# Three of four early weight conversions moved from the middle of an attention stage to its last steps

## The chip, the cores and the metric

One core of one Trainium2 chip runs the whole program. The metric is the device time of one execution in microseconds (us), less is better; the median of several runs is given.

## The reference

Sliding-window attention with four sink keys (2 batches, 8 heads, 768 positions, head size 64, window 128) is followed by two feed-forward layers over the 1536 tokens (512 wide, 2048 hidden). In short:

```python
keep = is_sink | in_window                      # 4 sinks, or 0 <= row - col < 128
x = softmax(where(keep, q @ k.T / 8, -1e9)) @ v # -> [1536, 512]
h = maximum(x @ w_in1, 0);  x = (h * h) @ w_out1
h = x @ w_in2;              out = (h * tanh(softplus(h))) @ w_out2
```

Inputs are drawn as 64-bit floats for the weights and 32-bit floats for q, k and v.

## The kernel before

**Attention.** A tile is one block of 128 rows of one batch (12 tiles); a pair is one tile and two heads, so there are 48 pairs, numbered 0 to 47. One loop over n from -3 to 51 (line 541) runs a software pipeline: in step n the scores of pair n+4 are made on PE (`emit_s`), their row maximum is taken on VectorE, DVE (`emit_max`, line 367), the exponentials of pair n+3 come from ScalarE, ACT (`emit_exp`, line 379), and in even steps the sums of the pairs n+1 and n+2 are inverted on DVE (`emit_rs`, lines 390 and 391) and multiplied in on GpSimd, POOL (`emit_norm`, line 399). PE transposes the probabilities (lines 407, 408; they are copied out of PSUM by DVE where the pair is the first of its tile, else by ACT, line 415) and multiplies them with the values (`emit_av`, line 428). When the last pair of a tile has gone through, the tile's output is split into a high and a low part: ACT writes `xh` (`emit_x`, line 477), then DVE writes `xl` (`split_x`, line 483). The output accumulates in a PSUM tile `av` that has a single buffer, so the first value matmul of the next tile waits for `xl` of the tile before. From step 44 on no new scores are made: steps 44 to 51 are the drain.

**Weights.** A weight block (128 hidden units of one matrix) arrives as 512 KB of 64-bit numbers in `raw` (three buffers) and is turned into two 32-bit parts by a `Conv` object. Its steps are: `load` (a DMA on SP's queue), `head_pool` (one POOL instruction, line 131), `mid_r` (two DVE instructions, lines 137 and 141), `mid_or` (one on DVE, line 147), `high` (one on ACT, line 162) and `low_pool` (one on POOL, line 166). A step's scratch comes from five buffers of 2 KB per partition. Four blocks are converted within attention: `wi` and `wo` of hidden block 0, then of hidden block 1 (conversions 0 to 3 below). Conversion m starts with its load at step 5 + 9m, and its other steps follow 5, 7, 8, 11 and 12 steps later.

**Feed-forward layers.** `moe` runs 96 slots of 24 matmuls: 12 of the first product (line 620, tile `h`) and 12 of the second (line 636, tile `o`), one slot behind. Slot 0's first product needs conversion 0, slot 1's first product conversion 2; the second products of slots 0 and 1 need conversions 1 and 3. In slots 0 to 13 two further blocks are converted per slot, with `head` on ACT (line 129), `mid` on DVE, `high` on ACT and `low` on DVE. The raw blocks for these are fetched three ahead, as soon as one of the three `raw` buffers is free.

**Order.** Both stages stand under `tc.manual_schedule()`: in the trace each engine's instructions of one stage run in the written order, in order and blocking. Instructions of the second stage, however, stand between those of the first where the built program put them: rows of line 620 appear on PE in the middle of the drain. Within a step the conversions come last (lines 598 to 601): what a conversion puts on DVE in step 44 or 45 stands ahead of `emit_rs` and `split_x` of step 46.

```python
for m, x in enumerate(blocks):
    step = CONV_STEPS.get(n - CONV_AT[0] - CONV_AT[1] * m)
    if step:
        getattr(x, step)()
```

Of the kernel before, what the change touches and what calls it, by code (L numbers as in the profile page):

```python
# [28 lines left out]
def kernel(  # L29
# [42 lines left out]
    def load_limits():  # L72
        for j, src in enumerate((n_sink, window)):
            nc.scalar.dma_start(out=raw_i[:, j, :], in_=src.bitcast(I32).partition_broadcast(1))

    def limits(ps):
        nc.vector.scalar_tensor_tensor(
            out=lim1, in0=raw_i[:, :, 1], scalar=4294967296.0, in1=raw_i[:, :, 0].bitcast(U32),
            op0=ALU.mult, op1=ALU.add,
        )  # L80
        nc.vector.tensor_scalar(lim1, lim1, 0.0, float(S), op0=ALU.max, op1=ALU.min)
        nc.tensor.matmul(ps, lhsT=one, rhs=lim1, start=True, stop=True)
        nc.vector.tensor_copy(lim, ps)
# [111 lines left out]
    def load_tile(t, names="qkv", halves=1):  # L195
        if t >= len(tiles):
            return
        b, i = tiles[t]
        hs = H // halves
        for nm in names:  # L200
            dst = {"q": qn, "k": kn, "v": vn}[nm]
            dst[b, i] = apool.tile([P, H, D], F32, tag=nm + "n", name=nm + "n", bufs=5 if nm == "v" else 3)
        for h in range(0, H, hs):
            for nm in names:
                src, dst = {"q": (q, qn), "k": (k, kn), "v": (v, vn)}[nm]
                nc.sync.dma_start(
                    out=dst[b, i][:, h : h + hs, :],
                    in_=src[b, h : h + hs, i * P : (i + 1) * P, :].rearrange("h p d -> p h d"),
                )
# [16 lines left out]
    def positions():  # L226
        make_identity(nc, ident)
        for dst, base, pattern, mult in (
            (rel, 0, [[-1, P]], 1), (col, 0, [[1, P]], 0), (relp, P, [[-1, P]], 1)
        ):  # L230
            nc.gpsimd.iota(
                dst, pattern=pattern, base=base, channel_multiplier=mult, allow_small_or_imprecise_dtypes=True
            )
            if dst is rel:
                nc.gpsimd.affine_select(
                    out=rel, in_=rel, pattern=pattern, base=base, channel_multiplier=mult,
                    compare_op=ALU.is_ge, fill=1.0e9,
                )
# [4 lines left out]
    def first_mask():  # L243
        outside(nc.vector, m_cur, rel, win_ap)
        nc.vector.scalar_tensor_tensor(
            out=mask0, in0=col, scalar=ns_ap, in1=m_cur, op0=ALU.is_ge, op1=ALU.mult
        )
# [17 lines left out]
    def load_vsink(b):  # L265
        vc[b] = apool.tile([P, D], F32, tag="vc", name="vc", bufs=2)
        nc.sync.dma_start(out=vc[b], in_=v[b, :, 0:SK, :])
# [26 lines left out]
    def prep(t, which, half=None):  # L294
        if t >= len(tiles):
            return
        b, i = tiles[t]
        js = slice(0, NPAIR) if half is None else slice(half * NPAIR // 2, (half + 1) * NPAIR // 2)
        src = (qn if which == "q" else kn)[b, i]
        pt = ps_p.tile([P, NPAIR, P], F32, tag="pt", name="tr")  # L300
        for j in range(js.start, js.stop):
            nc.tensor.transpose(  # L302
                pt[:, j, :], src[:, 2 * j : 2 * j + 2, :].rearrange("p h d -> p (h d)"), ident
            )
        if which == "q":
            if half in (None, 0):
                for d, nm in ((qh, "qh"), (ql, "ql")):
                    d[b, i] = apool.tile([P, NPAIR, P], F32R, tag=nm, name=nm, bufs=2)
            hi, lo = qh[b, i], ql[b, i]
        else:  # L310
            p0 = kpos(i)
            hi, lo = kh[:, :, p0 : p0 + P], kl[:, :, p0 : p0 + P]
        hi, lo, pt = hi[:, js], lo[:, js], pt[:, js]
        nc.scalar.copy(hi, pt)  # L314
        st["prep"] = (pt, hi, lo)
# [169 lines left out]
    blocks = []  # L485
# [1 line left out]
        wt[0, fb] = weight_tiles(w1pool, fb)  # L487
        blocks += [Conv(conv, 0, fb, part, wt[0, fb]) for part in ("wi", "wo")]
    WARM = (6, 3, 2, 1)
    CONV_AT = (5, 9)  # L490
    CONV_STEPS = {0: "load", 5: "head_pool", 7: "mid_r", 8: "mid_or", 11: "high", 12: "low_pool"}

    NPR = len(pairs)
    with tc.manual_schedule():
        load_limits()
        nc.scalar.preload_act_table_set("natural_log_exp_and_others")
        load_tile(0, "qk", halves=2)
        load_tile(1, "qk")
        load_tile(2, "kq")
        load_tile(0, "v")  # L500
        load_tile(3, "kq")
        positions()
        load_tile(1, "v")
        load_vsink(0)
        load_tile(2, "v")
        load_tile(3, "v")
        warm = apool.tile([P, P], F32, name="warm")
        nc.vector.memset(warm, 0.0)
        nc.vector.memset(one, 1.0)
        nc.gpsimd.memset(two, 2.0)  # L510
        for x in sums:
            nc.vector.memset(x, 1e-9)
        idle = ps_a.tile([P, P + 2], F32, tag="av", name="idle")

        def keep_warm(times):
            for _ in range(times):
                nc.tensor.matmul(idle[:, 0:P], lhsT=warm, rhs=warm, start=True, stop=True)  # L517

        keep_warm(WARM[0])
        limits(idle[:, P : P + 2])  # L520
        first_mask()
        prep(0, "q", 0)
        place_prep()
        keep_warm(WARM[1])
        prep(0, "k", 0)
        place_prep()
        keep_warm(WARM[2])
        emit_s(*pairs[0])
        emit_max(*pairs[0], 0)
        emit_max(*pairs[0], 1)  # L530
        prep(0, "q", 1)
        place_prep()
        prep(0, "k", 1)
        place_prep()
        emit_s(*pairs[1])
        emit_max(*pairs[1], 0)
        emit_max(*pairs[1], 1)
        second_mask()
        window_masks()
        emit_exp(*pairs[0])  # L540
        for n in range(-3, NPR + 4):
            at = {d: pairs[n + d] for d in range(-3, 5) if 0 <= n + d < NPR}
            last = {d for d in at if at[d][2] == NPAIR - 1}
            t, j = divmod(n, NPAIR)
            if 4 in at and n > -3:
                emit_s(*at[4])
            if 3 in at and n > -3:
                emit_exp(*at[3])
            if n % 2 == 0:
                group = [at[d] for d in (1, 2) if d in at]  # L550
                if group:
                    emit_rs(group)
                for p in group:
                    emit_norm(*p)
                    if p[2] == NPAIR - 1:
                        emit_sink(*p[:2])
            if -3 in last:
                emit_x(*at[-3][:2])
            if 4 in at and n > -3:
                emit_max(*at[4], 0)  # L560
                emit_max(*at[4], 1)
            split_x()


            if n % 2 == 0:
                if n >= 0:
                    prep(t + 2, "kq"[j // 2])
                for d in (-1, 0):
                    if d in at:
                        emit_t(*at[d])  # L570
                if -1 in last:
                    emit_sink_t(*at[-1][:2], st["s", *at[4]][0] if 4 in at else None)
            else:
                for d in (-3, -2):
                    if d in at:
                        emit_av(*at[d])
                if -2 in last:
                    emit_sink_mm(*at[-2][:2])
            if -1 in at:
                evac_t(*at[-1])  # L580
            if n in (-3, -2):
                prep(1, "qk"[n + 3])
            place_prep()
            evac_sink()
            if n >= 0 and j == NPAIR - 1:
                load_tile(t + 4, "q", halves=1 + (t + 5 == len(tiles)))
                load_tile(t + 4, "k")
                load_tile(t + 4, "v")
            if n == -1 or (n >= 0 and t < len(tiles) - 1 and (t % NB, j) == (NB - 1, 2)):
                sink_keys()  # L590
            if n < 0:
                keep_warm(WARM[3])
            if n == 1:
                fast_flag()
                load_vsink(1)
            if n in (5, 13):
                spread_vsink(n // 8)
            for m, x in enumerate(blocks):
                step = CONV_STEPS.get(n - CONV_AT[0] - CONV_AT[1] * m)
                if step:  # L600
                    getattr(x, step)()
    att.close()


# [421 lines left out]
```

## Time and profile before

| | |
|---|---|
| runs | median 633.4 us of 3 (633.07 to 634.25) |
| the profiled execution | 634.14 us, its span 632.4 us |
| busy share of the span | PE 99%, PE weight loads 82%, DVE 73%, ACT 58%, POOL 11% |
| chain that ended last | PE 96%, DVE 2%, ACT 1% |
| granted TensorE clock | 0.999 of full speed (the upper of its two levels) |

The span runs from the first to the last instruction; the profiled execution takes 1.7 us more than its span. Attention fills the first 106 us, the feed-forward layers the rest, in a steady alternation of 2.72 us of line 620 and 2.72 us of line 636. PE's busy share is modelled at the ends of its matmuls, so waits are better read from the distance between starts. A bracket at the end of a timeline row gives the idle time ahead of it and what ended it.

### The profile page before, as it was taken

To read this page: it belongs to the slowest core of one execution; us is meant where nothing else is said; L and a number is where in the kernel's file an instruction comes from. 1 tells how busy PE (TensorE), PEld (TensorE's weight loads), DVE (VectorE), ACT (ScalarE), POOL (GpSimd) and SP (SyncE) were. 2 spreads that over 40 slices of the span, in tenths; PEclk is the share of its full clock that TensorE was granted. 3 is DMA by queue.
4 is the path that set the end of the run, shared out by engine and by line. 5 is a ranking of instruction groups with operands and counts; after the bars stand their busy time and mean duration, and the time that the engine had idled before them with its cause. 6 is when DMAs were issued, how large, how long until landed. Compare 5 with 4: busy or idle time off the path is not lost.

```text
span 632.4 us, 9265 instructions
## 1 busy us (share of the span) xinstructions
PE 624.2 (99%) x3382; PEld 515.9 (82%) x3382; DVE 461.9 (73%) x968; ACT 363.7 (58%) x745; POOL 71.1 (11%) x97
## 2 busy tenths in 40 slices
PE   8999999999999999999999999999999999999996
PEld 7778787888888888888888888888888888888885
DVE  5988983999852011138889869999888888888884
ACT  5988985777744333347777745555454444544442
POOL 4686773000000000000000000000000000000000
PEclk9999999999999999999999999999999999999999
DMA  8644630666630000005666600000010000010001
GB/s 200 148 118 104 164 120 26 195 204 201 199 101 1 2 0 1 0 1 169 197 199 199 192 10 1 0 2 1 1 66 1 1 1 1 1 67 0 2 0 69
DMA packets 61189, 46.83 MB, mean 74 GB/s; under 512 B 38996, under 2 KB 55636, under 8 KB 61140
## 3 DMA queue, kind: packets, MB, share of 16 engines
q1 hardware_dynamic: 60848, 45.82, 25.0%
q8 instruction: 27, 0.44, 0.3%
q10 hardware_dynamic: 292, 0.39, 0.2%
q14 instruction: 22, 0.18, 0.1%
HBM read 43.06 MB, written 3.15 MB: 73 GB/s over the span
## 4 chain that ended last, share of the span: by engine, by line
PE 96%; DVE 2%; ACT 1%; issue 0%; DVEq 0%
PE h L620 41%; PE o L636 41%; PE s L356 4%; PE av L428 3%; PE tr L302 2%; PE pt L408 1%; PE pt L407 1%; PE idle L517 1%; PE av L464 1%; DVE s L367 1%; ACT pr L379 0%; DVE cv_a L147 0%; DVE cv_r L137 0%; ACT kh L314 0%; DVE cv_r L141 0%
## 5 line engine op out<-in xcount | busy, mean ns | idle before, releaser
L620 PE MATMUL h<-xl,wih 128*128 128x512 f32 x384 | 103.2, 390 | 0.0
L620 PE MATMUL h<-xh,wil 128*128 128x512 f32 x384 | 103.0, 390 | 0.0
L620 PE MATMUL h<-xh,wih 128*128 128x512 f32 x384 | 102.6, 389 | 0.0
L694 DVE TENSOR_TENSOR gl<-h,gh 128x512 fp32r<-128x512 f32 x48 | 33.2, 691 | 93.0 <-ACT gh L690 92.9
L620 PEld LDWEIGHTS h<-xl,wih 128*128 128x128 f32 x384 | 72.0, 188 | 15.2 <-issue 0.3
L620 PEld LDWEIGHTS h<-xh,wih 128*128 128x128 f32 x384 | 72.1, 188 | 15.0
L620 PEld LDWEIGHTS h<-xh,wil 128*128 128x128 f32 x384 | 71.9, 188 | 15.0 <-issue 0.2
L710 ACT ACTIVATE e<-t,small 128x512 f32<-128x512 f32 x48 | 34.8, 726 | 70.1 <-DVE t L706 70.1
L636 PE MATMUL o<-gh,wol 128*128 128x512 f32 x192 | 74.7, 389 | 0.0
L636 PE MATMUL o<-gl,woh 128*128 128x512 f32 x192 | 74.7, 389 | 0.0
L636 PE MATMUL o<-gh,woh 128*128 128x512 f32 x192 | 74.7, 389 | 0.0
L688 ACT ACTIVATE h<-h 128x512 f32<-128x512 f32 x48 | 27.9, 582 | 77.5 <-PE h L620 77.4
L636 PE MATMUL o<-wol,gh 128*128 128x512 f32 x176 | 68.5, 389 | 0.0
L636 PE MATMUL o<-woh,gl 128*128 128x512 f32 x176 | 68.5, 389 | 0.0
L636 PE MATMUL o<-woh,gh 128*128 128x512 f32 x176 | 68.5, 389 | 0.0
L726 ACT CAST gh<-t 128x512 fp32r<-128x512 f32 x44 | 27.4, 623 | 46.6 <-PE o L636 42.9
L399 POOL TENSOR_TENSOR pr<-pr,rs 128x544 f32<-128x544 f32 (+2 forms) x48 | 48.4, 1022 | 23.4 <-DVE rs L391 13.3
L147 DVE SCALAR_TENSOR_TENSOR cv_a<-cv_a,cv_r 128x512 int32<-128x512 int32 x64 | 44.4, 694 | 6.1
L379 ACT ACTIVATE pr<-s,nm 128x272 f32<-128x272 f32 (+2 forms) x96 | 44.4, 476 | 5.0 <-DVE nm L367 2.6
L731 DVE TENSOR_TENSOR gl<-t,gh 128x512 fp32r<-128x512 f32 x44 | 30.3, 690 | 19.8 <-ACT gh L726 19.8
L636 PEld LDWEIGHTS o<-gh,wol 128*128 128x128 f32 x192 | 36.1, 188 | 7.5
L636 PEld LDWEIGHTS o<-gl,woh 128*128 128x128 f32 x192 | 36.0, 188 | 7.5
(121 smaller groups left out, 1101.2 us busy)
## 6 DMA issues: line engine op xcount, KB each, us to landing
raw<-in_moe_w_in_dram SPq DMA_DIRECT2D x32, 512.0 KB, 3.8
raw<-in_moe_w_out_dram SPq DMA_DIRECT2D x32, 512.0 KB, 4.0
vn<-in_v_dram SPq DMA_DIRECT2D x12, 256.0 KB, 3.0
kn<-in_k_dram SPq DMA_DIRECT2D x11, 256.0 KB, 3.7
qn<-in_q_dram SPq DMA_DIRECT2D x10, 256.0 KB, 4.1
out_dram<-ob SPq DMA_DIRECT2D x8, 256.0 KB, 2.2
qn<-in_q_dram SPq DMA_DIRECT2D x4, 128.0 KB, 3.0
out_dram<-o SPq DMA_DIRECT2D x2, 256.0 KB, 2.9
```

The lines of the kernel that those rows point to most:

```text
L147: nc.vector.scalar_tensor_tensor(out=ai, in0=ai, scalar=3, in1=self.r, op0=ALU.logical_shift_left, op1=ALU.bitwise_or)
L356: nc.tensor.matmul(banks[e][:, 0:w], lhsT=x[b, i][r, j, :], rhs=y[r, j, c0 : c0 + w], start=(m == 0), stop=(m == 2),)
L379: nc.scalar.activation(out=pr[b, i][:, 2 * j + e, 0:w], in_=banks[e][:, 0:w], func=AF.Exp, bias=nm[:, e : e + 1], scale=-1.0, accum_out=sm ...
L399: nc.gpsimd.tensor_tensor(out=x, in0=x, in1=rs.to_broadcast([P, 2, w]), op=ALU.mult)
L428: nc.tensor.matmul(av[b, i][e * D : (e + 1) * D, j, :], lhsT=vn[b, kb][:, 2 * j + e, :], rhs=pts[:, c, e, :], start=(j == 0 and m == 0), s ...
L620: nc.tensor.matmul(ph, lhsT=w[a][:, d, :], rhs=x[:, d, :], start=(m == 0 and d == 0), stop=(m == 2 and d == NDC - 1),)
L636: nc.tensor.matmul(acc[sp][t], lhsT=a, rhs=x, start=(fb == 0 and m == 0), stop=(fb == NFB - 1 and m == 2),)
L688: nc.scalar.activation(out=ph, in_=ph, func=AF.Relu)
L694: nc.vector.tensor_tensor(out=gl, in0=hp.pop(n), in1=f32(gh), op=ALU.subtract)
L710: nc.scalar.activation(out=e, in_=t, func=AF.Ln, bias=two)
L726: nc.scalar.copy(g_tiles(n)[0], et[n][1])
L731: nc.vector.tensor_tensor(out=gl, in0=t, in1=f32(gh), op=ALU.subtract)
```

## The change

Conversion 0 keeps its steps. Conversions 1, 2 and 3 are loaded at steps 36, 37, 38 (before: 14, 23, 32) and their POOL heads stand at 41, 42 and 44 (before: 19, 28, 37). Their DVE, ACT and last POOL steps all stand in steps 44 to 47 (before: 21 to 26, 30 to 35 and 39 to 44). In steps with more than one, they are in the order of the conversions.

```diff
-    CONV_AT = (5, 9)
-    CONV_STEPS = {0: "load", 5: "head_pool", 7: "mid_r", 8: "mid_or", 11: "high", 12: "low_pool"}
+    CONV_STEPS = {}
+    for ops, ats in zip(
+        ("load", "head_pool", "mid_r", "mid_or", "high", "low_pool"),
+        ((5, 36, 37, 38), (10, 41, 42, 44), (12, 44, 44, 45), (13, 44, 45, 45), (16, 45, 46, 47), (17, 45, 46, 47)),
+    ):
+        for x, n in zip(blocks, ats):
+            CONV_STEPS.setdefault(n, []).append((x, ops))
...
-            for m, x in enumerate(blocks):
-                step = CONV_STEPS.get(n - CONV_AT[0] - CONV_AT[1] * m)
-                if step:
-                    getattr(x, step)()
+            for x, op in sorted(CONV_STEPS.get(n, []), key=lambda y: blocks.index(y[0])):
+                getattr(x, op)()
```

## Rows read from the trace of the kernel before

**Rows 1.** Page, part 4: the chain that ended last, by engine.
```profile
PE 96%; DVE 2%; ACT 1%; issue 0%; DVEq 0%
```

**Rows 2.** Windows: stretch; its length, busy PE, PEld, DVE, ACT, POOL, PEclk, DMA.
```profile
48.00:96.00 48.00, 47.53 (x539) 39.24 (x537) 43.11 (x166) 42.76 (x141) 34.38 (x38) 1.00 0.49 132
96.00:110.40 14.40, 14.40 (x136) 11.33 (x133) 3.72 (x13) 7.32 (x17) 4.99 (x6) 1.00 0.02 5
```

**Rows 3.** Timeline of PE, no conversion: start, us, engine, line, op, out<-in, count.
```profile
30.94 0.39 PE L356 MATMUL s<-kh,qh 64*128 64x272 f32 x2
...
31.51 1.09 PE L428 MATMUL av<-pts,vn 128*64 128x128 f32 x16
```

**Rows 4.** Timeline of PE between the second and the fourth conversion.
```profile
65.14 0.71 PE L356 MATMUL s<-kh,qh 64*128 64x272 f32 x2
...
66.03 0.66 PE L302 MATMUL tr<-ident,kn 128*128 128x128 f32 x4
...
75.83 0.70 PE L356 MATMUL s<-kh,qh 64*128 64x272 f32 x2
...
76.71 0.66 PE L302 MATMUL tr<-ident,qn 128*128 128x128 f32 x4
...
95.43 1.09 PE L428 MATMUL av<-pts,vn 128*64 128x128 f32 x16 [0.40 <-DVE xl L483]
```

**Rows 5.** Timeline of DVE in the drain.
```profile
97.70 0.29 DVE L455 COPY pst<-trs 128x128 f32<-128x128 f32 x1 [1.36 <-PE trs L449]
97.90 0.68 DVE L415 COPY pts<-pt 128x512 f32<-128x512 f32 x1
...
98.68 0.17 DVE L391 RECIPROCAL rs<-rs 128x2 f32<-128x2 f32 x1
101.04 0.69 DVE L483 TENSOR_TENSOR xl<-av,xh 128x512 fp32r<-128x512 f32 x1 [2.19 <-ACT xh L477]
```

**Rows 6.** Timeline of DVE in slot 0: one conversion's DVE part, up to its successor.
```profile
110.37 0.42 DVE L137 TENSOR_SCALAR cv_r<-raw 128x512 int32<-128x512 int32 x1
110.82 0.47 DVE L141 TENSOR_SCALAR cv_r<-raw 128x512 uint16<-128x512 uint32 x1
...
112.00 0.68 DVE L166 TENSOR_TENSOR wil<-cv_a,wih 128x512 fp32r<-128x512 f32 x1
```

**Rows 7.** Timeline of PE in the drain.
```profile
98.18 0.73 PE L620 MATMUL h<-xh,wil 128*128 128x512 f32 x2
...
101.15 0.71 PE L620 MATMUL h<-xh,wil 128*128 128x512 f32 x2
101.70 0.40 PE L620 MATMUL h<-xl,wih 128*128 128x512 f32 x1
102.03 1.09 PE L428 MATMUL av<-pts,vn 128*64 128x128 f32 x16
...
104.33 0.50 PE L620 MATMUL h<-xl,wih 128*128 128x512 f32 x1
```

**Rows 8.** Timeline of DVE and of POOL beside conversion 0's middle steps.
```profile
35.23 1.05 DVE L137 TENSOR_SCALAR cv_r<-raw 128x512 int32<-128x512 int32 x1
36.31 0.80 DVE L141 TENSOR_SCALAR cv_r<-raw 128x512 uint16<-128x512 uint32 x1
...
35.94 0.85 POOL L273 TENSOR_SCALAR_AFFINE_SELECT vs<-vc 128x512 f32<-128x512 f32 x1
```

**Rows 9.** Timeline of POOL: conversion 3's head and low, and the normalizations before.
```profile
83.25 1.54 POOL L131 TENSOR_SCALAR cv_a<-raw 128x512 f32<-128x512 f32 x1
...
96.48 2.15 POOL L399 TENSOR_TENSOR pr<-pr,rs 128x544 f32<-128x544 f32 x2 [0.20 <-DVE rs L391]
98.58 1.26 POOL L166 TENSOR_TENSOR wol<-cv_a,woh 128x512 fp32r<-128x512 f32 x1
```

**Rows 10.** Chain that ended last, in order of time: start, us, what.
```profile
106.29 4.30 PE h L620 x18
```

**Rows 11.** Timeline of SP: the last load of attention.
```profile
75.72 0.37 SPq L206 DMA_DIRECT2D vn<-in_v_dram  x1
```

## The prediction

> **What bounds it now.** I read the chain that ended last first: it is PE's for 96% [rows 1], so a microsecond counts only if PE waits less or more. Then the windows by stage: in the attention stretch from 48 to 96 us, where three of the four conversions lie, PE shows 47.5 of 48 us busy, DVE 43.1 and ACT 42.8; in the drain and slot 0 (96 to 110.4) PE stays full while DVE falls to 3.7 of 14.4 us [rows 2]. The change carries work from the first stretch, where DVE is nearly full, into the second, where it is nearly idle. Because a busy PE is modelled, I then read the starts on PE's timeline. A group of scores that waits for nothing is 0.57 us from its first start to the next work, 30.94 to 31.51 [rows 3]. Most of attention keeps this pitch, so PE itself limits most of it, and what the conversions cost there is only where the pitch is missed. Last, DVE's, POOL's and PE's timelines of the drain show who waits for whom.
>
> **The gain in the middle.** One group of scores takes 65.14 to 66.03, 0.89 us, another 75.83 to 76.71, 0.88 us, and a second of that kind follows before 81 us; value matmuls at 95.43 waited 0.40 us for `xl` [rows 4]. Against 0.57 us this is 0.32 + 0.31 + 0.31 + 0.40 = 1.3 us of PE waits that stand shortly behind work of the conversions 1 to 3. With that work gone I expect all of them to close: **-1.3 us**. Lower end 0: the waits have another cause, since pairs with narrow scores make DVE and ACT late by themselves. Upper end: the whole DVE work taken out. A conversion's DVE part runs from 110.37 to 112.00, 1.63 us to the start of its successor [rows 6]; three are 4.9 us. I take the value near the lower part because the PE waits are the nearest rows.
>
> **ACT and POOL, middle.** Three `high` leave ACT and three heads and lows leave POOL (1.54 and 1.26 us each [rows 9]). POOL had 13.6 of 48 us free [rows 2]; I count nothing beyond the waits above.
>
> **DMAs.** The three raw loads now stand on SP behind the last load of attention, issued at 75.72 [rows 11]. Two of their buffers have never been used and the third was freed by conversion 0, so nothing holds them back. Their first user is the moved head of step 41, four steps behind the head that stands at 83.25 before the change [rows 9], 8 us or more after the issue. No cost. The feed-forward loads, however, wait for the `mid_r` of conversions 1 to 3, now in the drain. Behind them SP holds only loads of the same kind. Their first user is the first feed-forward conversion; its DVE part (1.63 us) now falls into DVE's idle time between the drain and slot 0. If that cover were gone, 1.6 us of DVE would stand ahead of slot 2's weights. No cost taken.
>
> **The loss in the drain.** DVE runs in order. In steps 44 and 45 the new order puts three conversions' DVE parts behind the copy `pst` that ends at 97.99; behind them come the copy `pts`, the reciprocal for the last pair (together 97.90 to 98.85, 0.95 us) and `xl`, 0.69 us [rows 5]. Bare sum: 97.99 + 3 x 1.63 + 0.95 + 0.69 = 104.5. Before, `xl` ended at 101.04 + 0.69 = 101.73, since DVE idled 1.36 and 2.19 us [rows 5]. So `xl` is **2.8 us late at bare durations**. Who waits: the accumulator has one buffer, and the next tile's value matmuls started at 102.03 [rows 7], 0.3 us after `xl`. The last normalization on POOL waits for the same reciprocal, and ACT's `xh` stands behind the first `high`, but both are ready before `xl`.
>
> **Blocking between DVE and POOL.** Conversion 0's two `mid_r` instructions took 1.05 and 0.80 us where POOL's selects started at 35.94 [rows 8]; with POOL idle they take 0.42 and 0.47 [rows 6]. In the drain POOL is full: two normalizations (2.15 us) are behind the second head, the third head (1.54) follows, then the first `low` (1.26) [rows 9]. I expect the first `mid_r` to lose most of a normalization (1.0 of 1.08 us) to its first instruction, and the whole head less what has run (about 1.0) to its second, and a later step part of a low (0.5): 2.5 us. Lower end 0 (POOL has finished earlier); upper end all of one normalization, one head and one low, 3.9 us. I take 2.5, since rows 8 show a wait at each of the two instructions: `xl` is **5.3 us late**. The Trainium skill's page "SBUF — State Buffer", section "Who interferes with whom", says that a DVE copy or tensor_scalar in its two-port mode and any GpSimd instruction exclude each other for the whole of the one that issued first; rows 8 agree with their 1.05 and 0.80 us. By that rule the wait is the rest of the running POOL instruction and the loss is as in this forecast; by a rule of independent engines it would be the bare 2.8 us.
>
> **What PE can do meanwhile.** PE fills waits in the drain with slot 0's first product: 2 matmuls at 98.18, 3 from 101.15, 1 at 104.33 [rows 7]. 18 matmuls of slots 0 and 1 stand behind the drain, 4.30 us or 0.24 us each [rows 10]; 6 of them are slot 0's. These 6 can move up into the longer gap: -1.4 us. Slot 1's 12 need conversion 2's low part, on POOL behind the last normalization; I let 2 of them (0.4 us) into the drain's last wait. Loss: 5.3 - 1.4 - 0.4 = **+3.5 us**.
>
> **Sum.** +3.5 - 1.3 = +2.2 us. The profiled execution would take 634.14 + 2.2 = 636.3 us, its span 634.6. That execution lies 0.7 us above the median of 633.4, so the median would be 633.4 + 2.2 = **635.6 us**.
>
> **Rivals.**
> - *No blocking.* POOL is through with its head when DVE comes; `xl` is 2.8 us late, the loss 2.8 - 1.4 - 0.4 = 1.0, the sum 1.0 - 1.3 = -0.3: **633.1 us**. For it: conversion 3's row at 83.25 shows a head that takes 1.54 us with nothing in its way [rows 9]. Against it: in the new order two heads precede or follow the normalizations that PE needs.
> - *The middle was DVE's.* Place: steps 21 to 44. DVE's 43.1 of 48 us [rows 2] set the pace through buffers that come free late, and three conversions give back their full 4.9 us: 3.5 - 4.9 = -1.4, **632.0 us**, faster. It decides once the middle gives back over 4.8 us, or over 2.3 us if nothing blocks. For it: ACT is as full as DVE, and PE's waits there end on them. Against it: the constant 0.57 us [rows 3]. The Trainium skill's page "Perfetto Trace Analysis", section "Identifying the Most-Contended Engine", calls matmul busy time a poor measure and reads weight-load time instead. By that rule PE is 39.2 of 48 us used, DVE is the fuller one, and this rival holds; the starts on PE speak against it.
> - *PE has nothing to fill with.* The built order keeps slot 0's 6 matmuls behind the drain, or the first feed-forward head, waiting for its late load, holds up ACT: 5.3 - 1.3 = +4.0, **637.4 us**. For it: only 6 matmuls stood in the drain before. Against it: they stood in each of its waits.
> - *It doesn't do what it says.* The program's order, not the listing's, decides. In attention the rows of each engine keep the listed order, so I give this no chance of its own.
>
> **Numbers.** Forecast 0.45, no blocking 0.25, middle DVE's 0.2, nothing to fill 0.1. A measurement of this kernel tells 0.2%, 1.3 us, from no change. Faster by more: the second rival, 0.2. Within: no blocking, 0.25. Slower: forecast and last rival, 0.55. The range reaches from the second rival to the last, 631.9 to 637.4, and leaves out what lies beyond those two, under 2 in 10. The forecast's own range is 634.4 to 637.0: blocking between 1.3 and 3.9 us.
>
> **What would show it.** In the changed profile: the group at the former 75.83 back at 0.57 us (gain); `xl` of the tile before last behind nine conversion instructions, 3 to 6 us later against the last maximum (loss); `mid_r` rows over 0.8 us beside a POOL head (blocking); 8 or more of slot 0's matmuls in PE's gap ahead of the last tile's value matmuls (fill). The prediction is wrong if `xl` is not late, if PE finds other work there, or if the stretch up to the drain shrinks by more than 2 us.

## The result, and the profile after

The changed kernel takes 636.9 us (median of 6 runs, 636.37 to 637.57); the kernel before, run beside it on the same chip, 633.8 us (6 runs, 632.93 to 634.47). The ratio is 1.0051 (95% interval 1.0040 to 1.0062): **slower by 3.1 us**, more than the 0.2% that can be told from no change. The profiled execution of the changed kernel is one of 636.98 us with a span of 635.2 us.

PE's share of the chain that ended last is unchanged, 96% [rows 1]. First, after, the chain in order of time, from the last tiles of attention to slot 0's second product (start, length, what; x is the count of instructions):

```profile
96.39 0.29 DVE pst L455
...
104.36 0.34 DVE cv_r L137
...
104.77 0.60 DVE xl L483
105.41 1.13 PE av L428 x16
...
106.94 0.21 PE pt L408
...
111.13 2.76 PE h L623 x11
113.89 2.72 PE o L639 x12
...
617.09 13.61 PE o L639 x60
```

and the kernel before, the same view:

```profile
102.09 1.02 PE av L428 x16
...
103.60 0.11 PE pt L408
...
106.29 4.30 PE h L620 x18
110.60 2.72 PE o L636 x12
...
613.80 13.61 PE o L636 x60
```

From 96.39 on, for nine microseconds, the chain now runs through DVE, most of it conversion steps. Slot 0's second product starts at 113.89 in place of 110.60, 3.29 us later, and the last group of 60 matmuls at 617.09 in place of 613.80, again 3.29 us. (In these two traces the first `xl` stands at 23.41 and 23.43, so their clock times can be compared.) All of the difference is made before 114 us; from there on the feed-forward layers neither add nor win back anything. The spans differ by 2.8 us only, since the stretch from the last copy of the output to the end of the span also varies, from 3.6 to 5.3 us over all the traces (4.1 before, 3.7 after).

To part the gain from the loss I need a mark between them. The first `xl` starts anywhere from 22.5 to 23.45 us in different executions, whatever the kernel, so in general clock times of two traces can't be subtracted. Two distances can be compared: from the first `xl` (tile 0) to the one of tile 9, the last before the drain; and from there to the group of 48 first-product matmuls, the first long group that stands alike in all chains. DVE, kernel before:

```profile
23.41 0.69 DVE L483 TENSOR_TENSOR xl<-av,xh 128x512 fp32r<-128x512 f32 x1
...
89.10 0.42 DVE L137 TENSOR_SCALAR cv_r<-raw 128x512 int32<-128x512 int32 x1
...
94.60 0.69 DVE L483 TENSOR_TENSOR xl<-av,xh 128x512 fp32r<-128x512 f32 x1
```

DVE after, with what it did in the drain (bare durations and the idle times of before: [rows 5, 6]):

```profile
23.43 0.69 DVE L483 TENSOR_TENSOR xl<-av,xh 128x512 fp32r<-128x512 f32 x1
...
93.30 0.69 DVE L483 TENSOR_TENSOR xl<-av,xh 128x512 fp32r<-128x512 f32 x1
...
96.60 1.00 DVE L137 TENSOR_SCALAR cv_r<-raw 128x512 int32<-128x512 int32 x1
97.63 1.24 DVE L141 TENSOR_SCALAR cv_r<-raw 128x512 uint16<-128x512 uint32 x1
98.97 0.91 DVE L147 SCALAR_TENSOR_TENSOR cv_a<-cv_a,cv_r 128x512 int32<-128x512 int32 x1
99.80 0.69 DVE L137 TENSOR_SCALAR cv_r<-raw 128x512 int32<-128x512 int32 x1
...
101.48 1.18 DVE L147 SCALAR_TENSOR_TENSOR cv_a<-cv_a,cv_r 128x512 int32<-128x512 int32 x1
...
104.68 0.67 DVE L483 TENSOR_TENSOR xl<-av,xh 128x512 fp32r<-128x512 f32 x1
```

The middle takes 94.60 - 23.41 = 71.19 us before and 93.30 - 23.43 = 69.87 after: **1.32 us gained**. The drain, up to the group of 48 (369.00 before, 372.29 after, fences with the first runs below), takes 369.00 - 94.60 = 274.40 and 372.29 - 93.30 = 278.99: **4.59 us lost**. The balance, 3.27 us, is the 3.29 of the chain.

The row at 89.10 in the kernel before is not one of conversions 0 to 3: it is the first feed-forward conversion, whose load was early enough for the built program to put its three DVE instructions (89.10, 92.75 and 93.23) into attention. After the change its load is late and they stand in the drain, the first of them at 104.28, between the sum `rs` and its reciprocal, right ahead of `xl` (0.34 us of the chain). So the DVE work of four conversions left the middle, not of three.

POOL after, in the drain:

```profile
94.67 1.59 POOL L131 TENSOR_SCALAR cv_a<-raw 128x512 f32<-128x512 f32 x1
96.17 2.38 POOL L399 TENSOR_TENSOR pr<-pr,rs 128x544 f32<-128x544 f32 x2
98.52 1.70 POOL L131 TENSOR_SCALAR cv_a<-raw 128x512 f32<-128x512 f32 x1
```

The two normalizations stand behind the second head and run until 98.55. Both instructions of the first `mid_r` (96.60 to 97.60, 97.63 to 98.87) lie beside them; the third head lies beside the `mid_or` at 98.97 and the next `mid_r` at 99.80.

PE after, in the drain; the bracket is idle time before and what ended it:

```profile
99.03 1.18 PE L623 MATMUL h<-xh,wil 128*128 128x512 f32 x4
100.05 1.08 PE L623 MATMUL h<-xl,wih 128*128 128x512 f32 x4
100.97 1.08 PE L623 MATMUL h<-xh,wih 128*128 128x512 f32 x4
105.41 1.13 PE L428 MATMUL av<-pts,vn 128*64 128x128 f32 x16 [3.36 <-DVE xl L483]
```

All 12 of slot 0's first-product matmuls fit into the gap, and then PE still idles 3.36 us for `xl`. Behind that it is slow: a transpose holds the chain for 0.21 us, against 0.11 before, and from the 16 value matmuls to the long group of `h` it takes 111.13 - 105.41 = 5.72 us, against 106.29 - 102.09 = 4.20 for the same work before, 1.5 us more. The windows of these stretches (length, busy time of PE, PEld, DVE, ACT, POOL, then the granted clock, DMA share, GB/s) say why:

```profile
102.00:105.40 3.40, 0.05 (x1) 0.00 (x0) 3.26 (x9) 2.70 (x5) 0.67 (x2) 1.00 0.65 187
105.40:107.70 2.30, 2.29 (x21) 1.78 (x21) 2.15 (x3) 1.86 (x5) 2.24 (x3) 0.70 0.79 236
107.70:109.50 1.80, 1.80 (x10) 1.01 (x9) 1.57 (x2) 0.51 (x1) 1.71 (x2) 0.50 0.64 244
109.50:111.00 1.50, 1.50 (x25) 1.39 (x24) 1.36 (x3) 0.00 (x0) 0.00 (x0) 0.92 0.05 14
```

After its idle time PE is granted 0.70, then 0.50 of full speed, the lower level of 1.2 GHz, and is back near the upper level of 2.4 GHz by 111 us; 0.70 and 0.92 are means of stretches in which the level changes.

### The profile page after: what moved, and what is told of

It reads as the page before. It is cut to its first block, busy times and chain, and to the rows that moved or that the text cites. A ratio compares the mean times of both kernels' runs of the same rounds, so it can differ in the third digit from the quotient of the medians.

```text
span 635.2 us, 9270 instructions
## 1 busy us (share of the span) xinstructions
PE 624.6 (98%) x3382; PEld 516.8 (81%) x3382; DVE 467.3 (74%) x968; ACT 364.5 (57%) x745; POOL 71.2 (11%) x97
## 4 chain that ended last, share of the span: by engine, by line
PE 96%; DVE 2%; ACT 0%; issue 0%; DVEq 0%
PE o L639 41%; PE h L623 41%; PE s L356 4%; PE av L428 3%; PE tr L302 2%; PE pt L408 1%; PE pt L407 1%; PE idle L522 1%; PE av L464 1%; DVE cv_a L147 1%; DVE cv_r L137 1%; DVE cv_r L141 0%; ACT kh L314 0%; DVE xl L483 0%; DVE s L367 0%
## 5 line engine op out<-in xcount | busy, mean ns | idle before, releaser
L623 PE MATMUL h<-xh,wil 128*128 128x512 f32 x384 | 103.4, 391 | 0.0
L639 PEld LDWEIGHTS o<-gh,woh 128*128 128x128 f32 x192 | 36.0, 188 | 7.5
```

What stands on the lines that cost most here:

```text
L623: nc.tensor.matmul(ph, lhsT=w[a][:, d, :], rhs=x[:, d, :], start=(m == 0 and d == 0), stop=(m == 2 and d == NDC - 1),)
L639: nc.tensor.matmul(acc[sp][t], lhsT=a, rhs=x, start=(fb == 0 and m == 0), stop=(fb == NFB - 1 and m == 2),)
```

## The experiments

The diffs below are cut to the rows of step numbers that change, out of six: loads, heads, `mid_r`, `mid_or`, `high`, `low`, each for conversions 0 to 3. Run 7 is compared with run 4's rows, run 10 with run 7's, run 9 with the kernel before; the others start from the changed kernel (of runs 4 and 8 the new rows alone are shown). "Distance" is the first `xl` to tile 9's (71.19 before, 69.87 after), "drain" the stretch from there to the group of 48 (274.40 before, 278.99 after); the rows of the marks of one run:

```profile
372.29 10.88 PE h L623 x48
```

(after) and

```profile
369.00 10.88 PE h L620 x48
```

(before). The kernel before, run beside them, took 633.62 us with runs 1 to 4, 633.5 with runs 5 to 8 and 633.64 with runs 9 and 10.

**1. Is the loss the wait for `xl`?** Conversions 2 and 3 give up their place ahead of the `xl` of the tile before last and come one step later.

```diff
- (12, 44, 44, 45), (13, 44, 45, 45), (16, 45, 46, 47), (17, 45, 46, 47)
+ (12, 44, 46, 46), (13, 44, 46, 46), (16, 45, 47, 47), (17, 45, 47, 47)
```

> As the changed kernel, but only conversion 1's DVE steps stay in step 44; those of conversions 2 and 3 move to step 46, behind the xl of the tile before last, and their high and low to step 47. Queue theory (what costs is that three conversions stand ahead of xl on DVE): xl ends about 3.5 us earlier than in the changed kernel, the value matmuls after it start near 102 us instead of 105.4, PE's gap there is filled and no lower clock follows; the middle keeps its gain of 1.3 us. The second copy pst and conversion 2's low are now late instead, up to 1 us. Sum: 632.5 to 633.8 us, 3 to 4 us below the changed kernel. Rival (conversions in the drain cost what they cost, wherever they stand in it): 636 to 637 us.

Measured: 635.09 us (11 runs), ratio 1.0024 (1.0016 to 1.0033), 1.3 us above the range expected. Distance 69.85, drain 277.38: 1.6 of the 4.6 us are back. DVE and ACT of this run:

```profile
100.10 0.69 DVE L483 TENSOR_TENSOR xl<-av,xh 128x512 fp32r<-128x512 f32 x1 [0.30 <-ACT xh L477]
106.26 0.28 DVE L455 COPY pst<-trs 128x128 f32<-128x128 f32 x1
```

```profile
106.38 0.62 ACT L162 CAST woh<-cv_a 128x512 fp32r<-128x512 f32 x1 [2.43 <-DVE cv_a L147]
```

`xl` starts 100.10 - 22.5 = 77.6 us behind the first `xl`, as before (101.04 - 23.41) and 3.7 us sooner than after (104.68 - 23.43 = 81.25). But the two conversions, with the first `mid_r` of the first feed-forward one among them, now stand ahead of the copy `pst` of the last tile, which ends at 106.54, and ACT's `high` of conversion 3 waits 2.43 us for DVE with the last copy `pts` behind it (106.90). PE's last value matmuls need both. The wait was moved from `xl` to `pst` and `pts`, and less than expected came back. PE's longest waits are shorter here (1.58 and 1.06 us), and its granted clock stays at 1.00 from 96 to 111 us, so much of the 1.6 us can be the slow stretch that is gone; this run doesn't part the two.

**2. Is part of it POOL?** The three heads go to odd steps up to 39, where POOL has free time, and their loads ahead of them; DVE's steps stay.

```diff
- ((5, 36, 37, 38), (10, 41, 42, 44), (12, 44, 44, 45),
+ ((5, 28, 29, 30), (10, 35, 37, 39), (12, 44, 44, 45),
```

> As the changed kernel, but the loads of conversions 1 to 3 stand in steps 28 to 30 and their POOL heads in steps 35, 37 and 39, so that no head runs beside a DVE conversion step in the drain. Blocking theory (a DVE conversion step waits for the POOL instruction that runs): the first mid_r's second instruction falls from 1.24 to about 0.5 us, xl ends about 1 us earlier, total 1 to 1.5 us less: about 635.7 us. Rival (these instructions are slow there for another reason, or the heads only move the wait): mid_r stays at 1.0 and 1.24 us, total 636.9 us. If the heads cost PE in the middle, the drain starts later than at 95.15 us by what they cost.

Measured: 635.15 us (6 runs), ratio 1.0031 (1.0019 to 1.0042). Distance 69.85 (the heads cost nothing in the middle), drain 278.03, 0.96 us shorter than after.

```profile
94.47 2.15 POOL L399 TENSOR_TENSOR pr<-pr,rs 128x544 f32<-128x544 f32 x2 [0.72 <-DVE rs L391]
```

```profile
95.66 1.24 DVE L137 TENSOR_SCALAR cv_r<-raw 128x512 int32<-128x512 int32 x1
96.94 0.46 DVE L141 TENSOR_SCALAR cv_r<-raw 128x512 uint16<-128x512 uint32 x1
```

With no head ahead of them the two normalizations are done at 96.62, so only the first `mid_r` instruction still waits behind one; the second is at its bare 0.46. The `mid_or` and the `mid_r` behind it are at their bare durations too (0.69 and 0.42, against 0.91 and 0.69 beside the third head after the change). So the heads' place on POOL is worth about 1 us of the loss: the second head through the normalizations that it delays, the third directly. PE's clock falls in this run as it does after the change (0.52 from 103.4 to 105.5 us, behind 2.34 us of idle time), so the difference isn't the clock's.

**3. What does the lower clock cost?** After the change, in step 47 and ahead of the waiting value matmuls, PE gets eight matmuls whose product nothing reads.

```diff
+ if n == 47:
+     gap = ps_p.tile([P, 512], F32, tag="pt", name="gap")
+     w1 = wt[0, 1]["wih"]
+     for _ in range(8):
+         nc.tensor.matmul(gap, lhsT=w1[:, 0, :],
+             rhs=w1.rearrange("p c f -> p (c f)"), start=True, stop=True)
```

> As the changed kernel, with 8 dummy products (0.23 us each, of weights that ScalarE has just written) on PE ahead of the value matmuls that wait for xl. They use idle PE time; the built order then lets 9 instead of 13 matmuls of slots 0 and 1 into the drain, which by itself costs 4 x 0.23 = 0.9 us. Clock theory (after 3.4 us of idle PE the granted clock fell to the lower level and the next matmuls took twice as long, 1.4 us in all): the granted clock stays near 1 from 105 to 109.5 us, transposes are again 0.11 us apart, total about 0.5 us less than the changed kernel: 636.4 us. Rival (the slow pitch comes from the loads that land there, or from waits): transposes stay 0.21 us apart, total about 0.9 us more: 637.8 us.

Measured: 637.42 us (6 runs), ratio 1.0063 (1.0050 to 1.0075); run again beside the changed kernel, 637.49 against 637.11 (runs 5 and 6). A window and the chain of run 3:

```profile
105.40:107.70 2.30, 2.30 (x30) 1.80 (x29) 1.81 (x3) 0.58 (x1) 2.24 (x3) 1.00 0.77 226
```

```profile
103.33 2.14 PE gap L583 x8
105.47 1.02 PE av L428 x16
...
106.75 0.11 PE pt L408
...
109.67 3.67 PE h L630 x15
```

With PE at work ahead of them the same transposes run 0.11 us apart at a granted clock of 1.00, with nearly as many bytes landing beside them (226 GB/s against 236), and the stretch from the 16 value matmuls to the long group of `h` takes 109.67 - 105.47 = 4.20 us, as in the kernel before. The drain is 278.47, only 0.52 us shorter than after, because four real matmuls that had stood in the gap (0.9 us) now come behind it: by this balance 0.5 + 0.9 = 1.4 us is what the lower clock took, by the stretch 1.5. Over whole executions the granted clock is 0.995 to 0.997 in all 11 of the changed kernel and 0.998 or more in 10 of the 11 filled ones, so the fall isn't that of one profile.

In the total the half microsecond doesn't show: in the two filled profiles the last copy of the output is done 0.5 and 1.1 us sooner (631.01 and 630.50 against 631.55 and 631.56; in the second, 0.5 us of this is an earlier start, its first `xl` at 22.99), but the span ends 4.5 and 5.3 us behind that copy in place of 3.7 and 3.6. In the traces of all the other kernels this is 3.6 to 4.3 us; why it is longer here I did not find out. So the clock's price is read from the trace's starts and not confirmed by a time.

**4. A better order for the same move.** From runs 1 and 2: conversions 1 to 3 in the order in which their products are needed (the one of slot 1's first product before the two second products), heads early, DVE's steps spread over steps 44, 46 and 48.

```diff
+ ((5, 29, 28, 30), (10, 39, 37, 41), (12, 46, 44, 48),
+  (13, 46, 44, 48), (16, 47, 45, 49), (17, 47, 45, 49))
```

> The moved conversions placed by when they are due and where DVE waits: conversion 2 (due first) in step 44, conversion 1 in step 46 behind xl, conversion 3 in step 48 behind the second pst; heads in steps 37, 39 and 41, loads in steps 28 to 30. Queue theory: xl is at most 1 us later against the start of the drain than before the change, PE fills that wait, no lower clock; middle gain of 1.3 us kept: 632.0 to 633.3 us, 0.5 to 1.8 us below the kernel before. Rival (the drain costs as much as the middle saves): 633.8 us or above.

Measured: 633.54 us (11 runs), ratio 0.9998 (0.9990 to 1.0007), 0.2 us above the range expected; drain 275.55, only 1.15 above before. What is left stands for a good part on ACT and POOL; ACT's rows:

```profile
98.89 0.62 ACT L162 CAST wih<-cv_a 128x512 fp32r<-128x512 f32 x1 [2.48 <-DVE cv_a L147]
99.42 0.57 ACT L477 CAST xh<-av 128x512 fp32r<-128x512 f32 x1
```

`xh` waits behind a `high` that waited for DVE, and on POOL the last normalization (100.83) behind a `low` (99.59) that waited 2.24 us for the `high`.

**5 and 6. The changed kernel and run 3 once more, side by side.**

> The changed kernel once more, to compare on one chip with the run that keeps PE busy and with the runs beside it: 636.5 to 637.3 us, ratio to the kernel before 1.004 to 1.006.

> The changed kernel with 8 dummy products ahead of the value matmuls once more. Clock theory: 0.5 us less than the changed kernel beside it, since 1.4 us of slow matmuls go and 0.9 us of filling is lost. Rival (no gain in time): equal or more.

Measured: 637.11 us, ratio 1.0062 (1.0049 to 1.0075), drain 279.03; and 637.49, ratio 1.0061 (1.0048 to 1.0074), drain 278.40. The drain is 0.6 us shorter with the filling, the time is not; for the time the rival of run 6 held.

**7. Highs and lows one step later,** so that `xh` and the normalization go first:

```diff
- (16, 47, 45, 49), (17, 47, 45, 49))
+ (16, 48, 46, 50), (17, 48, 46, 50))
```

> The conversions placed by due time, but their high and low moved behind what the drain needs of ACT and POOL: conversion 2's high behind xh and its low behind the last normalization (step 46), conversion 1's in step 48, conversion 3's in step 50. Queue theory, now for ACT and POOL too (high ahead of xh costs 0.5 us of xl, low ahead of the last normalization 1 us): out of 1.15 us that the drain is still longer than before the change, 0.6 to 1 go; 632.6 to 633.2 us, faster than the kernel before by 0.4 to 1.0 us. Rival (DVE alone sets it): 633.5 us as without this step.

Measured: **632.8 us** (12 runs), ratio 0.9990 (0.9982 to 0.9999). Distance 69.83, drain 274.95, 0.55 above before. By the interval it is faster than the kernel before, by 0.1%; that is less than the 0.2% set as what can be told.

```profile
97.33 0.59 ACT L477 CAST xh<-av 128x512 fp32r<-128x512 f32 x1 [1.69 <-PE av L464]
```

Now `xh` waits for its own value matmuls alone, and the `high` stands behind it, at 98.45. The time is in the range expected.

**8. Only two conversions moved,** conversion 1 back in the middle, since the distances by tile showed that it costs nothing there.

```diff
+ ((5, 14, 28, 30), (10, 19, 37, 39), (12, 21, 44, 46),
+  (13, 22, 44, 46), (16, 25, 46, 48), (17, 26, 46, 48))
```

> Conversion 1 stays in the middle where it was before the change (its removal moved no time between the tiles' xl there); only conversions 2 and 3 are moved, to steps 44 and 46, with high and low behind what the drain needs. If the middle's gain comes from conversions 2 and 3 alone, xl of the last tile ahead of the drain stays about 69.9 us behind that of the first (71.2 before the change), and the drain has one conversion less: 632.2 to 633.0 us. Rival (the first feed-forward conversion, whose load comes early again, goes back into the middle and takes 0.6 us): 633.0 to 633.6 us.

Measured: 633.51 us (11 runs), ratio 0.9999 (0.9990 to 1.0008); missed. The time is in the rival's range, but not for the rival's reason: the distance is 69.91 as hoped, and the drain is 275.58, longer than run 7's:

```profile
100.97 1.49 DVE L137 TENSOR_SCALAR cv_r<-raw 128x512 int32<-128x512 int32 x1
```

This row is the first feed-forward conversion's. The built program put it ahead of the last moved step and of `pst` (103.32); in run 7 it stands behind `pst` (103.55 and 102.55). With less work in the drain the next stage's comes in sooner, at a worse place.

**9. Is it DVE's work that costs in the middle?** The kernel before, where conversions 1 to 3 do `mid_r` a second time (0.9 us of DVE each, with the same result).

```diff
  getattr(x, step)()
+ if step == "mid_r" and m > 0:
+     x.mid_r()
```

> The kernel before, with the first DVE step (two instructions, 0.9 us) of conversions 1, 2 and 3 issued a second time in the middle of attention: 2.7 us more DVE work there, nothing else. If DVE's work is what conversions 2 and 3 cost in the middle, the last xl ahead of the drain stands 0.5 to 1.8 us later behind the first than the 71.2 us of before, nothing of it at conversion 1, and the total is 634.1 to 635.4 us. Rival A (ACT's or POOL's steps of the conversions cost it): 71.2 us and 633.6 us. Rival B (DVE sets the pace of the whole middle): 2.7 us more, 636.3 us.

Measured: 635.54 us (7 runs), ratio 1.0030 (1.0019 to 1.0042). Distance 96.43 - 23.31 = 73.12, 1.93 above before, both 0.1 us above the ranges expected; drain 274.44, as before.

```profile
23.31 0.69 DVE L483 TENSOR_TENSOR xl<-av,xh 128x512 fp32r<-128x512 f32 x1
96.43 0.69 DVE L483 TENSOR_TENSOR xl<-av,xh 128x512 fp32r<-128x512 f32 x1
```

By tile 5, behind conversion 1, 0.17 us is left of its 0.9; conversion 2 adds 0.97 up to tile 7, and another 0.8 comes by tile 9. So DVE work costs about its full time at conversions 2 and 3, and little at conversion 1, where there is slack.

**10. Run 7 with conversion 1's `mid_or` behind the copy `pst`,** and conversion 3's `mid_r` and `mid_or` one step later.

```diff
- (12, 46, 44, 48), (13, 46, 44, 48),
+ (12, 46, 44, 49), (13, 48, 44, 49),
```

> As the kernel with ACT and POOL steps freed, but the second DVE step of conversion 1, which waited there for a POOL low and held up the second pst copy, stands behind that copy (step 48), and conversion 3's DVE steps one step later (49). Queue theory: pst is 0.5 to 1 us earlier, the drain 0.2 to 0.5 us shorter, total 632.3 to 632.7 us. Rival (PE is already full there, or conversion 3's low is late for slot 1's second product): 632.8 us or more.

Measured: 632.99 us (11 runs), ratio 0.9991 (0.9982 to 1.0000), drain 274.99: nothing gained over run 7, as the rival had it. The 0.5 us still left in the drain are not explained.

## Why the prediction was right, and where its sizes were off

**Right in sign and course; the size came out by errors that partly cancel.** 635.6 was forecast and 636.9 measured, just inside the forecast's own range. As a change, +2.2 us was forecast and +3.1 measured (3.3 by the chain). The rows named in advance are there: `xl` late behind nine moved conversion instructions (and one of the feed-forward's), `mid_r` rows over 0.8 us, more than 8 of slot 0's matmuls in the gap, a group in the middle back at 0.57 us. One sign came with another neighbour than forecast: the slow `mid_r` rows stand beside the normalizations, not beside a head.

**The gain: 1.3 forecast, 1.32 measured, but not all from the pieces named; that the sum fits so well is luck.** PE after, in the first two named places:

```profile
65.12 0.71 PE L356 MATMUL s<-kh,qh 64*128 64x272 f32 x2
66.02 0.65 PE L302 MATMUL tr<-ident,kn 128*128 128x128 f32 x4
...
75.81 0.39 PE L356 MATMUL s<-kh,qh 64*128 64x272 f32 x2
76.38 0.66 PE L302 MATMUL tr<-ident,qn 128*128 128x128 f32 x4
```

The second closed (0.57 us), the first did not (0.90): its wait was not conversion 1's. The other two closed as well (a group at 79.44 to 80.01, and no wait at the value matmuls of 94.13). By tile, measured from tile 0, conversion 1's removal gave nothing up to tile 6 (46.92 before, 46.89 after), 0.7 us came by tile 7, where conversion 2 had stood (54.55, 53.85), and another 0.6 by tile 9. So 0.32 of the sum was wrongly put down to a conversion, and about as much came from waits that I had not listed. Run 8 confirms that conversion 1 costs nothing there. By tile 9 both conversion 3 and the first feed-forward conversion had stood in the kernel before; no run parts these two.

**`xl`: 5.3 us late forecast, 4.9 measured.** Its end would have stood at 101.73 - 1.30 = 100.43 and stands at 104.68 + 0.67 = 105.35. Of the blocking, 2.5 us were forecast, and the rows lose 2.3: 1.00 at the first `mid_r` instruction for a bare 0.42 and 1.24 at the second for 0.47, then 0.91 for 0.69 and 0.69 for 0.42 beside the third head, and 1.18 for 0.69 at a `mid_or` beside the first `low` on POOL, the part of a `low` that was forecast:

```profile
100.62 1.49 POOL L166 TENSOR_TENSOR wol<-cv_a,woh 128x512 fp32r<-128x512 f32 x1 [0.41 <-ACT woh L162]
```

The sum fits, the partner at the second `mid_r` instruction does not: it was to wait for the head, about 1.0 us, and lost 0.77 beside the second normalization, which the head ahead of it had pushed late; the third head took 0.22 and 0.27 from the next two instead. Together with the bare 2.8 us and the feed-forward's 0.34, these waits would make 5.4; neighbours on DVE overlap a little (the copy `pts` starts at 100.89, before the step ahead of it ends at 101.00), and 4.9 is left. The Trainium skill's "SBUF — State Buffer", "Who interferes with whom", also says that a DVE instruction with two SBUF inputs contends with a GpSimd instruction that reads SBUF; the `mid_or` at 101.48, which has two, agrees with its 1.18 us.

**The fill: 1.8 us forecast, 1.7 measured.** Before, 18 of the 24 matmuls of slots 0 and 1 stood behind the drain; after, 11. That is seven moved up, at 0.24 us each, where eight were forecast (eight at 0.24 us are 1.9, so the forecast's own sum is 0.1 us off).

**What was missing: the clock.** 4.9 - 1.7 = 3.2 us, and the drain lost 4.6. The missing **1.4 us** are PE's lower clock behind its idle 3.4 us, as the windows show it at 0.70 and 0.50 and run 3 shows it gone. The forecast let PE idle this long and priced what followed at full speed. This term, 1.4 us, less the 0.4 that `xl` came sooner than forecast, is what put the forecast about 1 us too low. The Trainium skill's "TensorE: Matmul & The Clock Gate", Part 1, has an idle PE fall to 1.2 GHz; the 0.50 agrees, and I had not used it.

**The rivals.** *No blocking* fell: rows of 1.00 and 1.24 us, and run 2 gave back 0.96 us by moving heads alone. *The middle was DVE's* was half right in kind: run 9 shows that added DVE work costs time there once the slack is gone. But of the 4.9 us (6.5 with the feed-forward conversion that went too) only 1.3 came back, far under the 4.8 from which it would have decided. By the Trainium skill's "Perfetto Trace Analysis", "Identifying the Most-Contended Engine", DVE was the engine to relieve; here the starts on PE were the better measure. *Nothing to fill* fell: 12 matmuls went into the gap, before PE idled.

**Costs taken as none.** Loads and heads in the middle cost nothing that shows (distance 69.85 with early heads), and no later slot waits for the late feed-forward loads (3.29 us from slot 0 to the end). But the first feed-forward conversion, which the forecast put into DVE's idle time behind the drain, came into the drain and took 0.34 us ahead of `xl`. ACT was not free of waits: the first `high` stood waiting 3.30 us ahead of `xh`, and the last normalization on POOL waited 2.73 us for `rs`. Behind the late `xl` neither counted; in runs 1 and 4, with an earlier `xl`, the same kind of wait became the limit.

## What to carry to other kernels

Idle time of an engine in a drain is not free room: the instructions run in the written order, and what is put there delays the short step queued behind it that releases the next engine. Place such work by what stands behind it on every engine it touches (here the copies and `xl` on DVE, `xh` and `pts` on ACT, the normalization on POOL): the same three conversions cost 3.1 us or, in run 7's order, nothing (632.8 us against 633.5). Where a forecast lets PE idle for some microseconds, price what follows from rows at the lower granted clock too.

## What the runs showed of the hardware that was not expected

PE, full up to 102 us and then idle for 3.4 us, was granted 0.70 in 105.4 to 107.7, 0.50 in 107.7 to 109.5 and 0.92 in 109.5 to 111; with filling matmuls from 103.33 on it stayed at 1.00. In run 2, behind 2.34 us of idle time, it was granted 0.52 in 103.4 to 105.5 and 0.54 in 105.5 to 107; in run 1, with waits of 1.58 and 1.06 us, it stayed at 1.00. The waits between DVE and POOL go both ways: while DVE waited up to 0.8 us in one instruction ahead of `xl`, POOL's head took 1.70 us beside DVE's steps and 1.54 without [rows 9], its `low` 1.49 against 1.26. And the start of the whole program shifts by up to 0.9 us between executions (first `xl` at 22.5 to 23.45), so that traces are compared by distances from a common mark.
